# Split f32r operands in ten first products of an attention and feed-forward kernel, with low parts added by DMA

## The chip, the core and the metric

The kernel runs on one core of a Trainium2 chip. The metric is the device time of one launch in microseconds, the median of several runs. The engines are TensorE (PE, matmuls; PEld its weight loads), VectorE (DVE), ScalarE (ACT), GpSimd (POOL) and SyncE (SP), which only issues DMAs here. Each engine works through its own instructions in order and waits on semaphores for the others.

## What is computed

The reference runs three stages on 1536 tokens (two batches of 768) of width 512:

```python
scores = scale * np.matmul(q, k.transpose(0, 1, 3, 2)) + bias     # 8 heads, local window of 96 and 8 global keys
attn = softmax(where(keep, scores, -1e9)) @ v
x = attn as (1536, 512)
h = x @ w_in                                                      # 512 -> 2048
g = h * np.tanh(np.log1p(np.exp(h)))                              # above 20: log1p(exp(h)) = h
x = g @ w_out                                                     # 2048 -> 512
for e in range(4):                                                # experts, p normalised over e
    out += p[:, e:e + 1] * (np.maximum(x @ w1[e], 0.0) @ w2[e])
```

The first feed-forward weights `w_in` and `w_out` arrive as 64-bit numbers.

## The kernel before

The tokens are worked on in three blocks of 512. Block 0 passes attention, the first feed-forward layer (FFN) and most of the experts; blocks 1 and 2 do their attention in between and follow. The change lies in block 0's FFN.

That FFN has 16 steps of 128 hidden channels. Step `s` needs its weights: SP loads 1 MB of 64-bit words into one of four buffers (`fetch`; `big0`, `big1`, and `raw0`, `raw1`, which hold attention inputs at other times), ACT takes the absolute value of the upper words, scaled (L603), and three DVE instructions put a 32-bit number together (L606, L608, L610). The result is a tile `w` of 128x1024: columns 0 to 511 for the first product, 512 to 1023 for the second. SP also stores it to `wfirst` in HBM for later blocks. The first product `hidden_first` (L771) multiplies f32 operands: four blocks of 128 rows, x in the tile `x0`, into a PSUM bank `h`; in the trace an f32 matmul appears as two, so one product is 8 rows. The gate follows: exponent on ACT (L660), cap on DVE (L664), square, logarithm and exponential on ACT (L668, L673, L674), and three DVE instructions (L679, L683, L687) that leave the gated values in `gl` or `gh`. The second product `project_first` (L784) adds them through `w` into the banks `acc0` to `acc3`; the last two steps share one such projection. All this is f32. Later FFN blocks and the experts split operands into a high part rounded to f32r and a low part, and take three f32r products: high by high, high by low, low by high (L644, `hidden`).

The order of all this is a string of letters, `PLAN`, written out by hand. One letter is one instruction or a few, and each engine carries out its own in the order of the string. `t` is one of the three DVE instructions of a conversion (48 letters), `a` ACT's first instruction of one, `H` a first product, `e c n l u v g` the parts of a gate, `P` a projection and `Q` the last one, of steps 14 and 15. `i` loads four attention inputs of block 1, `j` splits queries and keys, `1` to `6` are the pieces of the attention of block 1 for one pair of heads (2 scores, 3 softmax, 4 scaling and splitting of later inputs, 5 transpose, 6 product with the values), and `w` is a third of the splitting of expert weights (a high part on ACT, two low parts). `TURN` names the buffer of each step's load. A load is issued as soon as the step that used its buffer before has been converted, and takes its place in SP's queue.

After `Q`, the results go into y0 and step 16, the first expert, begins.

Of the kernel before, what the change touches and what calls it, by code (L numbers as in the profile page):

```python
# [9 lines left out]
F32 = mybir.dt.float32  # L10
F32R = mybir.dt.float32r
I32 = mybir.dt.int32
I64 = mybir.dt.int64
AF = mybir.ActivationFunctionType
ALU = mybir.AluOpType

P = 128
B, H, S, D = 2, 8, 768, 64
# [4 lines left out]
TB = 512  # L23
NB = NTOK // TB
KC = DM // P
NF1 = 16
# [15 lines left out]

PLAN = (
    "SSYXXESYSEXSEDXNXESNTDCTXSENAZNEXATTSCZEDAXANSFSNEXTTDCNEZAXANTETSCZaADXNAtSFNTEXSCTXEAZSEDAVSVaXTTX"
    "CSEZAEADVVFTXTCEZAAaDVVTtTCaAZtAFtHttttHetctntlHtauevgHcattnltPeuvagcetPntltauHvgctntlPteauvgHctntlt"
    "aPuevgctnPtltauvHgttatPectntltHauvgtPetctnltHtauvgaHtectntlHteauvgPcetntltHwuvgctnPtltieuvHgcwnwlPeu"
    "vgcnljHwjuvgwP12ecnlwHuvg34612Pecnl3uvg5Hw4w6w12Pecnl3uvg54P6Q"
)

AFTER = {  # L50
# [2 lines left out]
}  # L53


TURN = [0, 1, 2, 3] * (NF1 // 4)
FREE = {2: 4, 3: 8}
EXTRA = 15,

# [99 lines left out]
class Pair:  # L159
# [17 lines left out]
    def split(self):  # L177
        pass
# [361 lines left out]
class Body:  # L540
# [35 lines left out]
    def fetch(self, s):  # L576

        kind, t, n = self.steps[s]
        if kind == "ffn" and self.wide and t == 0:
            self.w64[s] = (self.big + self.twice)[TURN[n]].bitcast(I64)  # L580
            if n > 0 or not self.loaded:
# [185 lines left out]

    def hidden_first(self, s):
        self.h[s] = ps = self.bank(f"h{s}")
        for kc in range(KC):  # L770
            self.nc.tensor.matmul(ps, self.w32[s][:, kc * P:(kc + 1) * P], self.x0[:, kc, :], start=kc == 0, stop=kc == KC - 1)  # L771

    def gate_first(self, s):
        self.g[s] = self.temp("gl" if s % 2 else "gh", s, bufs=3)
# [254 lines left out]
    def first_block(self, ready, now):  # L1029


        nc = self.nc
        pairs = [FirstPair(self, k) for k in range(TB // P * NP)]
        then = Attention(self, self.pair, 1, NB - 1)
        n = dict.fromkeys("SXEDNTCAFHecnluvgPatw", 0)
        narrowing = [self.narrow(c) for c in range(NF1)]
        parts = [self.part(c) for c in range(NF1, NF1 + 3)]
        self.x0 = self.xy.tile([P, KC, TB], F32, tag="xyh", name="x0")

        for pair in pairs:  # L1040
            pair.load()
# [3 lines left out]
        def ahead():  # L1045
            while ready["fetch"] < NF1:
                c = ready["fetch"]
                before = [m for m in range(c) if TURN[m] == TURN[c]][-1:]
                if n["S"] < FREE.get(TURN[c], 0) or any(n["t"] < 3 * m + 3 for m in before):
                    break  # L1050
                now("fetch", c + 1)
# [24 lines left out]
            return run  # L1076

        def hidden(s):
            if s == 10:
                for c in range(NF1, NF1 + 3):  # L1080
                    self.fetch(c)
            assert n["F"] == 4 and n["t"] >= 3 * s + 3
            self.accumulating = True
            self.hidden_first(s)
            ahead()
            self.nc.sync.dma_start(self.wfirst[s], self.w32[s])
# [4 lines left out]
        def last(k):  # L1091
            assert n["P"] == NF1 - 2 and n["g"] == NF1
            self.project_first(NF1 - 2, NF1 - 1)

        def begin(c):
            assert (c < 2 or n["A"] >= min(2 * c - 2, len(pairs))) and (c < 10 or n["P"] > c - 10)
            next(narrowing[c])
# [7 lines left out]
        def part(k):  # L1105
            c, third = divmod(k, 3)
            assert ready["fetch"] >= NF1 and n["S"] == len(pairs) and n["P"] >= 8 + 2 * c
            if third == 0:
                ready["fetch"] = NF1 + 3
                next(parts[c])  # L1110
            try:
                parts[c].send("vector" if third else None)
            except StopIteration:
                pass

        def begin_next(k):
            assert n["t"] == 3 * NF1
            then.load(4)

        pair = lambda stage, *args: lambda k: getattr(pairs[k], stage)(*args)  # L1120
# [1 line left out]
            "S": scores, "X": pair("biased"), "E": pair("exps"), "D": inverse, "N": scale(nc.gpsimd), "V": scale(nc.vector), "T": pair("trans"),  # L1122
            "C": pair("copy", nc.scalar.copy), "Z": pair("copy", nc.vector.tensor_copy), "A": pair("av"),
            "F": take(nc.scalar.copy), "G": take(nc.vector.tensor_copy), "a": begin, "t": convert, "w": part,
            "Y": warm, "H": hidden, "e": self.mish_exp, "c": self.mish_cap, "n": self.mish_n, "l": self.mish_r,
            "u": self.mish_u, "v": self.mish_v, "g": self.gate_first, "P": project, "Q": last,
            "i": begin_next, "j": lambda k: then.split(k + 1),
            "1": lambda k: then.ahead(), "2": lambda k: then.scores(), "3": lambda k: then.softmax(),
            "4": lambda k: (then.norm(), then.parts()), "5": lambda k: then.trans(), "6": lambda k: then.av(),
        }  # L1130
# [199 lines left out]
```

## Time and profile before

| | |
|---|---|
| median of 3 runs | 883.1 us (882.48 to 883.12) |
| profiled execution | 882.74 us, span 880.9 us |
| PE busy | 869.7 us of the span (99%) |
| DVE, ACT, POOL busy | 569.9, 482.3, 388.6 us |
| first product of step 0 to end of `Q` | 37.5 to 150.4 us |
| chain of work that ended last | PE 94% of the span |

Shares of the whole span are means over unlike stages: DVE is at 65% overall and at 98% in the stretch of the changed steps. The granted clock of PE is 1.00 (of 2.4 GHz) in every window read here.

### The profile page before, as it was taken

The page shows a single profiled execution, that of the slowest core. Times are in us where ns is not written, and L with a number is a line of the kernel's source. Part 1 is how long each engine was busy: PE and PEld are TensorE (multiplying, and loading weights), DVE is VectorE, ACT ScalarE, POOL GpSimd, SP SyncE. Part 2 cuts the span into 40 slices and gives each one's busy share as a digit, 9 for nine tenths or more (in the row PEclk, how much of TensorE's full clock was granted, in tenths as well). Part 3 has the DMA queues.
Part 4 walks back from the last instruction along what each step waited for, and adds up shares of the span by engine and source line. Part 5 has one row for each costly group of instructions (what it writes and reads, how often), then busy time and mean ns, then how long its engine had stood idle before and what let it go on. Part 6 is the DMA issues. An engine that isn't in the chain of part 4 may idle for free.

```text
span 880.9 us, 11248 instructions
## 1 busy us (share of the span) xinstructions
PE 869.7 (99%) x3848; PEld 669.2 (76%) x3848; DVE 569.9 (65%) x1112; ACT 482.3 (55%) x943; POOL 388.6 (44%) x416
## 2 busy tenths in 40 slices
PE   9899999999999999999999999999999999999997
PEld 5544445888888888888888888788888888888886
DVE  6999977866678674566656667645455555555555
ACT  6665665878777775577675567533333333333330
POOL 4000020777777776555310225554445555544420
PEclk9999999999999999999999999999999999999999
DMA  9488834444435432887555640611111112111002
GB/s 323 168 330 257 320 127 148 143 147 169 164 126 183 148 143 73 308 291 288 221 197 195 244 168 0 185 56 49 48 48 48 48 54 65 50 48 48 1 1 99
DMA packets 39858, 126.15 MB, mean 143 GB/s; under 512 B 4080, under 2 KB 6896, under 8 KB 37744
## 3 DMA queue, kind: packets, MB, share of 16 engines
q1 hardware_dynamic: 39648, 125.32, 40.6%
q8 instruction: 32, 0.52, 0.2%
q14 instruction: 34, 0.28, 0.1%
q10 hardware_dynamic: 144, 0.02, 0.0%
HBM read 97.02 MB, written 28.31 MB: 142 GB/s over the span
## 4 chain that ended last, share of the span: by engine, by line
PE 94%; DVE 2%; DMA 1%; ACT 0%; POOL 0%; issue 0%; ACTq 0%; POOLq 0%; DVEq 0%
PE acc_l L944 20%; PE h L644 20%; PE acc L732 20%; PE ha L893 9%; PE hx L893 7%; PE h L771 6%; PE acc L784 6%; PE pt L201 2%; PE o L308 2%; PE s L262 1%; PE s L261 1%; DMA qk<-in_qk 1%; PE s L365 0%; PE o L403 0%; DVE raw L843 0%; DVE t3l L822 0%
## 5 line engine op out<-in xcount | busy, mean ns | idle before, releaser
L629 POOL TENSOR_TENSOR wl<-w,wh 128x512 fp32r<-128x512 f32 x90 | 118.7, 1339 | 59.9 <-ACT wh L626 57.4
L797 DVE SCALAR_TENSOR_TENSOR big<-acc_l,prob,big 128x512 f32<-128x512 f32 x120 | 88.8, 746 | 79.0 <-PE acc_l L944 78.8
L876 POOL TENSOR_TENSOR zl<-wout,zh 128x512 fp32r<-128x512 f32 x32 | 40.8, 1297 | 85.1 <-ACT zh L874 85.1
L876 POOL TENSOR_TENSOR sumsl<-bias,sumsh 128x512 fp32r<-128x512 f32 x32 | 42.9, 1364 | 69.2 <-ACT sumsh L874 69.2
L679 DVE SCALAR_TENSOR_TENSOR nr<-e,n 128x512 f32<-128x512 f32 x48 | 33.1, 690 | 48.3 <-ACT n L674 48.3
L906 ACT COPY raw<-ha 128x512 f32<-128x512 f32 x33 | 19.4, 587 | 79.6 <-PE ha L893 79.6
L660 ACT ACTIVATE e<-h 128x512 f32<-128x512 f32 x48 | 28.1, 586 | 61.1 <-PE h L644 25.5
L196 POOL TENSOR_SCALAR p<-p,st 128x256 f32<-128x256 f32 (+1 forms) x58 | 42.0, 735 | 39.9 <-ACT v L250 35.0
L771 PE MATMUL h<-x,w 128*128 128x512 f32 x128 | 56.8, 593 | 0.7 <-ACT x L408 0.7
L732 PE MATMUL acc<-wh,gh 128*128 128x512 f32 x128 | 52.5, 410 | 0.0
L286 ACT ACTIVATE p<-t,st 128x256 f32<-128x256 f32 (+1 forms) x96 | 46.3, 484 | 8.1 <-DVE st L275 8.0
L944 PE MATMUL acc_l<-zh,gh 128*128 128x512 f32 x128 | 50.7, 396 | 0.0
L626 ACT CAST wh<-w 128x1024 fp32r<-128x1024 f32 x48 | 50.2, 1046 | 0.7
L644 PE MATMUL h<-y0h,wh 128*128 128x512 f32 x128 | 50.6, 395 | 0.0
L944 PE MATMUL acc_l<-zh,gl 128*128 128x512 f32 x128 | 50.5, 394 | 0.0
L944 PE MATMUL acc_l<-zl,gh 128*128 128x512 f32 x128 | 50.4, 394 | 0.0
L644 PE MATMUL h<-y0l,wh 128*128 128x512 f32 x128 | 50.3, 393 | 0.0
L732 PE MATMUL acc<-wh,gl 128*128 128x512 f32 x128 | 50.2, 392 | 0.0
L644 PE MATMUL h<-y0h,wl 128*128 128x512 f32 x128 | 50.2, 392 | 0.0
L944 PE MATMUL acc_l<-zh,gl_late 128*128 128x512 f32 (+1 forms) x128 | 50.0, 391 | 0.0
L275 DVE CUSTOM_DVE_ANT_0 t<-s,bias 128x256 f32<-128x256 f32 (+1 forms) x96 | 34.5, 399 | 24.0 <-PE s L262 20.8
L944 PE MATMUL acc_l<-zh,gh_late 128*128 128x512 f32 (+1 forms) x128 | 50.0, 391 | 0.0
(232 smaller groups left out, 2489.7 us busy)
## 6 DMA issues: line engine op xcount, KB each, us to landing
w<-in_wts SPq DMA_DIRECT2D x32, 512.0 KB, 4.6
raw<-in_qkv SPq DMA_DIRECT2D x32, 512.0 KB, 3.6
big<-in_wff SPq DMA_DIRECT2D x8, 1024.0 KB, 6.8
raw<-in_wff SPq DMA_DIRECT2D x8, 1024.0 KB, 8.2
wfirst<-w SPq DMA_DIRECT2D x16, 512.0 KB, 8.1
w<-wfirst SPq DMA_DIRECT2D x16, 512.0 KB, 4.5
wkeep<-wh SPq DMA_DIRECT2D x16, 512.0 KB, 3.6
wkeep<-wl SPq DMA_DIRECT2D x16, 512.0 KB, 2.9
```

What stands on the lines that cost most here:

```text
L196: engine.tensor_scalar(self.p[:, j, 0:self.nk * P], self.p[:, j, 0:self.nk * P], st[:, 2 + j:3 + j], 0.0, ALU.mult, ALU.add)
L286: nc.scalar.activation(p[:, j, 0:n], t[:, j, 0:n], AF.Exp, bias=self.least[:, j:j + 1], scale=-1.0, accum_out=self.sum[:, j:j + 1])
L626: (nc.vector.tensor_copy if copy == "vector" else nc.scalar.copy)(hi, w)
L629: getattr(nc, engine or "gpsimd").tensor_tensor(lo[:, c], w[:, c], hi.bitcast(F32)[:, c], ALU.subtract)
L644: nc.tensor.matmul(ps, a[:, c], r[:, kc, :], start=m == 0, stop=m == 3 * KC - 1)
L732: nc.tensor.matmul(acc[:, h], a, r, start=opens and k == 0 and m == 0, stop=closes and k == len(chunks) - 1 and m == 2)
L771: self.nc.tensor.matmul(ps, self.w32[s][:, kc * P:(kc + 1) * P], self.x0[:, kc, :], start=kc == 0, stop=kc == KC - 1)
L784: self.nc.tensor.matmul(acc, w[k][:, 512 + d * P:512 + (d + 1) * P], g[k], start=s == 0, stop=s == NF1 - 1)
L797: nc.vector.scalar_tensor_tensor(o, acc, p, o, ALU.mult, ALU.add)
L876: nc.gpsimd.tensor_tensor(lo[:, c], w[:, c], hi.bitcast(F32)[:, c], ALU.subtract)
L893: nc.tensor.matmul(ps, a[:, c], r[:, kc, :], start=opens and n == 0, stop=n == 5, skip_group_check=True)
L944: nc.tensor.matmul(o, a[:, c], r[:, w], start=n == 0, stop=n == 5)
```

## The change

From step `WHOLE` = 6 on, the first product takes split operands. x is split once: for each of its four blocks ACT copies the high part (`x0h`) and DVE subtracts it from x (`x0l`); letters `b`, eight. For each of steps 6 to 15 the first half of `w` is split by letter `s`: ACT writes minus w, rounded to f32r, into a tile half `halfl`; a DMA issued from POOL adds w itself to that tile in place, which leaves the low part; ACT writes the rounded w into `halfh`. There are four such slots, so step `s` takes the one of step `s` - 4. The product is then 12 f32r matmuls in place of four f32 ones, with the low part of the weights in the last four.

```diff
-TURN = [0, 1, 2, 3] * (NF1 // 4)
+TURN = [0, 1, 2, 3] * 3 + [0, 1] * 2
+WHOLE = 6
...
     def hidden_first(self, s):
         self.h[s] = ps = self.bank(f"h{s}")
-        for kc in range(KC):
-            self.nc.tensor.matmul(ps, self.w32[s][:, kc * P:(kc + 1) * P], self.x0[:, kc, :], start=kc == 0, stop=kc == KC - 1)
+        w = self.w32[s]
+        if s < WHOLE:
+            for kc in range(KC):
+                self.nc.tensor.matmul(ps, w[:, kc * P:(kc + 1) * P], self.x0[:, kc, :], start=kc == 0, stop=kc == KC - 1)
+            return
+        (wh, wl), (xh, xl), m = self.halves[s % KC], self.x[0], 0
+        for a, r in ((wh, xh), (wh, xl), (wl, xh)):
+            for kc in range(KC):
+                self.nc.tensor.matmul(ps, a[:, kc * P:(kc + 1) * P], r[:, kc, :], start=m == 0, stop=m == 3 * KC - 1)
+                m += 1
+
+    def split_first(self, s):
+
+        nc, w, (wh, wl) = self.nc, self.w32[s][:, 0:512], self.halves[s % KC]
+        nc.scalar.activation(wl, w, AF.Copy, scale=-1.0)
+        nc.gpsimd.dma_start(wl.bitcast(F32), w, accum_op=ALU.add)
+        nc.scalar.copy(wh, w)
...
+        self.x[0] = self.block("x0")
+        halves = [self.xy.tile([P, KC, TB], F32R, tag="xyl", name=f"half{p}") for p in "hl"]
+        self.halves = [[half[:, k, :] for half in halves] for k in range(KC)]
...
-            if s == 10:
+            if s == 9:
                 for c in range(NF1, NF1 + 3):
                     self.fetch(c)
...
+        def x_part(k):
+            assert n["F"] == 4
+            (xh, xl), at = [x[:, k // 2, :] for x in self.x[0]], self.x0[:, k // 2, :]
+            if k % 2:
+                nc.vector.tensor_tensor(xl, at, xh.bitcast(F32), ALU.subtract)
+            else:
+                nc.scalar.copy(xh, at)
...
-                parts[c].send("vector" if third else None)
+                parts[c].send("vector" if third and c < 1 else None)
...
-            assert n["t"] == 3 * NF1
+            assert n["t"] >= 36
             then.load(4)
...
+            "b": x_part, "s": split,
```

`PLAN` is written anew as well. Four of the six low parts of letter `w` go from DVE to POOL. Steps 12 to 15 load into `big0` and `big1` in turn, so that `raw0` and `raw1` are free for block 1's attention inputs after step 11. Three places show what the new order moves.

DVE, around the gate of step 4 (`gh` in L687 before, L688 now). The conversion that stands there (`w_696` before, `w_701` now) is that of step 7; `x0l` is the low part of x. Before:

```order
L664 TENSOR_SCALAR n_722<-e_721 128x512
L606 TENSOR_SCALAR w_696<-w_696 128x1024
L608 SCALAR_TENSOR_TENSOR w_696<-raw_123,w_696 128x1024
L610 SCALAR_TENSOR_TENSOR w_696<-raw_123,w_696 128x1024
L679 SCALAR_TENSOR_TENSOR nr_751<-e_721,n_722 128x512
L683 SCALAR_TENSOR_TENSOR nr_751<-nr_751,n_722 128x512
L687 SCALAR_TENSOR_TENSOR gh_757<-nr_751,h_700 128x512
```

Now:

```order
L1118 TENSOR_TENSOR x0l<-x_173,x0h 128x512
L665 TENSOR_SCALAR n_727<-e_726 128x512
L1118 TENSOR_TENSOR x0l<-x_173,x0h 128x512
L607 TENSOR_SCALAR w_701<-w_701 128x1024
L680 SCALAR_TENSOR_TENSOR nr_755<-e_726,n_727 128x512
L684 SCALAR_TENSOR_TENSOR nr_755<-nr_755,n_727 128x512
L1118 TENSOR_TENSOR x0l<-x_173,x0h 128x512 x2
L688 SCALAR_TENSOR_TENSOR gh_770<-nr_755,h_705 128x512
L609 SCALAR_TENSOR_TENSOR w_701<-raw_123,w_701 128x1024
L611 SCALAR_TENSOR_TENSOR w_701<-raw_123,w_701 128x1024
```

Four subtractions of x stand among these, and two of the conversion's instructions have moved behind the gate.

ACT, at the gates of steps 14 and 15 (`e_1057` and `e_1119` before, `e_1165` and `e_1196` now), with the attention of block 1 around them: `p` is an exponential, `pt` the copy of a transpose, `qs`, `kh` and `v` casts of later inputs, `wh` an expert weight. Before:

```order
L660 ACTIVATE e_1057<-h_1015 128x512
L668 ACTIVATE e_1057<-n_1058 128x512
L673 ACTIVATE n_1058<-e_1057 128x512
L674 ACTIVATE n_1058<-n_1058 128x512
L286 ACTIVATE p_1_1064,st_1_1066<-t_1_1065,st_1_1066 128x256 x2
L298 CAST pt_0_1081<-pt_0_1076 128x4x128
L626 CAST wh_1090<-w_871 128x1024
L235 CAST qs_3_1097<-raw_123 128x256
L237 CAST kh_3_1099<-raw_123 128x512
L250 CAST v_1_1104<-raw_122 128x2x2x64
L660 ACTIVATE e_1119<-h_1084 128x512
```

Now:

```order
L661 ACTIVATE e_1165<-h_1127 128x512
L669 ACTIVATE e_1165<-n_1166 128x512
L674 ACTIVATE n_1166<-e_1165 128x512
L675 ACTIVATE n_1166<-n_1166 128x512
L236 CAST qs_2_1176<-raw_123 128x256
L238 CAST kh_2_1178<-raw_123 128x512
L251 CAST v_0_1183<-raw_122 128x2x2x64
L661 ACTIVATE e_1196<-h_1151 128x512
L669 ACTIVATE e_1196<-n_1197 128x512
L674 ACTIVATE n_1197<-e_1196 128x512
L675 ACTIVATE n_1197<-n_1197 128x512
L287 ACTIVATE p_1_1208,st_1_1210<-t_1_1209,st_1_1210 128x256 x2
```

Before, the exponentials of pair 1 and the copy of pair 0's transpose stood between the two gates; now those exponentials stand behind both. On PE the order from there on is first product 14, first product 15, a score, projection 12, transpose of pair 0, projection 13, a score, transpose of pair 1, the product with the values, `Q`. Before, first products 14 and 15 had a score, projection 11 and a transpose between them.

SP, from the load of step 13 on (`big` and `raw` from `in_wff` are the loads of steps, `w` from `in_wts` those of experts, `raw` from `in_qkv` attention inputs). Before, `raw_122` and `raw_123` from `in_wff` are steps 14 and 15:

```order
L582 DMA big_125<-in_wff 128x1024
L582 DMA raw_122<-in_wff 128x1024
L1086 DMA wfirst<-w_696 128x1024
L582 DMA raw_123<-in_wff 128x1024
L1086 DMA wfirst<-w_724 128x1024
L1086 DMA wfirst<-w_745 128x1024
L587 DMA w_867<-in_wts 128x1024
L587 DMA w_869<-in_wts 128x1024
L587 DMA w_871<-in_wts 128x1024
```

Now, the last `big_124` and `big_125` are steps 14 and 15:

```order
L583 DMA big_125<-in_wff 128x1024
L1105 DMA wfirst<-w_701 128x1024
L1105 DMA wfirst<-w_729 128x1024
L588 DMA w_893<-in_wts 128x1024
L588 DMA w_895<-in_wts 128x1024
L588 DMA w_897<-in_wts 128x1024
L1105 DMA wfirst<-w_757 128x1024
L230 DMA raw_122<-in_qkv 128x1024 x2
L230 DMA raw_123<-in_qkv 128x1024 x2
L583 DMA big_124<-in_wff 128x1024
L1105 DMA wfirst<-w_773 128x1024
L583 DMA big_125<-in_wff 128x1024
```

The loads of the last two steps have gone behind the expert weights and the attention inputs. On POOL eight of the ten adding DMAs stand ahead of everything else of this stretch, and the last two (steps 14 and 15) behind the splitting of two queries and keys.

## Rows read from the trace of the kernel before

**Rows 1.** The page, busy us and share of the span by engine.
```profile
PE 869.7 (99%) x3848; PEld 669.2 (76%) x3848; DVE 569.9 (65%) x1112; ACT 482.3 (55%) x943; POOL 388.6 (44%) x416
```
**Rows 2.** Windows: PE, PEld, DVE, ACT, POOL busy us; clock, DMA share, GB/s.
```profile
75.00:100.00 25.00, 25.00 (x60) 11.12 (x59) 24.45 (x32) 14.18 (x19) 0.00 (x0) 1.00 0.90 295
100.00:125.00 25.00, 25.00 (x62) 11.31 (x62) 21.09 (x29) 14.73 (x25) 4.92 (x4) 1.00 0.59 212
```
**Rows 3.** Timeline of PE: start, duration, instruction, count; first f32, then f32r.
```profile
75.36 3.60 PE L771 MATMUL h<-x,w 128*128 128x512 f32 x8
78.79 3.60 PE L784 MATMUL acc<-gl,w 128*128 128x512 f32 x8
...
168.41 0.39 PE L644 MATMUL h<-y0h,wh 128*128 128x512 f32 x1
...
171.17 0.28 PE L261 MATMUL s<-kh,qs 128*128 128x256 f32 x1
```
**Rows 4.** Timeline of DVE: gate of step 4, cap, conversion, gate of step 5.
```profile
68.88 0.69 DVE L679 SCALAR_TENSOR_TENSOR nr<-e,n 128x512 f32<-128x512 f32 x1
...
70.93 0.42 DVE L664 TENSOR_SCALAR n<-e 128x512 f32<-128x512 f32 x1
71.26 0.69 DVE L606 TENSOR_SCALAR w<-w 128x1024 int32<-128x1024 int32 x1
...
74.39 0.68 DVE L679 SCALAR_TENSOR_TENSOR nr<-e,n 128x512 f32<-128x512 f32 x1
...
75.83 0.69 DVE L687 SCALAR_TENSOR_TENSOR gl<-nr,h 128x512 f32<-128x512 f32 x1
```
**Rows 5.** Groups by shape, 0 to 265 us: count, busy us, mean ns, idle before.
```profile
L626 ACT CAST wh<-w 128x1024 fp32r<-128x1024 f32 x19 | 20.0, 1050 | 0.4
L242 DVE TENSOR_TENSOR kl<-raw,kh 128x512 fp32r<-128x512 f32 x20 | 16.6, 831 | 0.6
L237 ACT CAST kh<-raw 128x512 fp32r<-128x512 f32 x22 | 13.6, 620 | 0.0
L299 DVE TENSOR_TENSOR pt<-pt,pt 128x512 fp32r<-128x512 f32 x16 | 11.1, 691 | 11.6 <-ACT pt L298 11.6
L668 ACT ACTIVATE e<-n 128x512 f32<-128x512 f32 x16 | 10.1, 630 | 24.1 <-DVE n L664 24.1
L660 ACT ACTIVATE e<-h 128x512 f32<-128x512 f32 x16 | 9.5, 591 | 11.4 <-PE h L771 11.1 <-DVE nr L679 0.3
...
L196 DVE TENSOR_SCALAR p<-p,st 128x256 f32<-128x256 f32 x6 | 1.9, 351 | 0.1
```
**Rows 6.** Timeline of DVE: cap and last gate instruction of step 15.
```profile
138.51 0.42 DVE L664 TENSOR_SCALAR n<-e 128x512 f32<-128x512 f32 x1
...
142.41 0.69 DVE L687 SCALAR_TENSOR_TENSOR gl<-nr,h 128x512 f32<-128x512 f32 x1
```
**Rows 7.** Timeline of PE: product 15, projection 12, a transpose, the last projection.
```profile
131.67 3.60 PE L771 MATMUL h<-x,w 128*128 128x512 f32 x8
...
135.58 3.60 PE L784 MATMUL acc<-gh,w 128*128 128x512 f32 x8
139.01 0.60 PE L201 MATMUL pt<-ident,p 128*128 128x128 f32 x4
...
143.35 1.02 PE L784 MATMUL acc<-gh,w 128*128 128x512 f32 x2
```
**Rows 8.** DMA issues at 68.5, 92 and 102 us: KB each, median us to landing.
```profile
raw<-in_wff SPq DMA_DIRECT2D x1, 1024.0 KB, 7.3
...
wfirst<-w SPq DMA_DIRECT2D x2, 512.0 KB, 12.3
...
raw<-in_qkv SPq DMA_DIRECT2D x4, 512.0 KB, 4.8
```
**Rows 9.** Timelines of POOL and DVE where both work; idle before in brackets.
```profile
117.42 0.89 POOL L240 TENSOR_TENSOR qs<-raw,qs 64x256 fp32r<-64x256 f32 x1 [93.66 <-DMA wfirst<-w]
...
117.75 1.11 DVE L683 SCALAR_TENSOR_TENSOR nr<-nr,n 128x512 f32<-128x512 f32 x1
```

More of the change, by code (lines that the diff above doesn't have):

```diff
@@ L44 @@
     "SSYXXESYSEXSEDXNXESNTDCTXSENAZNEXATTSCZEDAXANSFSNEXTTDCNEZAXANTETSCZaADXNAtSFNTEXSCTXEAZSEDAVSVaXTTX"
-    "CSEZAEADVVFTXTCEZAAaDVVTtTCaAZtAFtHttttHetctntlHtauevgHcattnltPeuvagcetPntltauHvgctntlPteauvgHctntlt"
-    "aPuevgctnPtltauvHgttatPectntltHauvgtPetctnltHtauvgaHtectntlHteauvgPcetntltHwuvgctnPtltieuvHgcwnwlPeu"
-    "vgcnljHwjuvgwP12ecnlwHuvg34612Pecnl3uvg5Hw4w6w12Pecnl3uvg54P6Q"
+    "CSEZAEADVVFTXTCEZAAaDVVTtTCaAZtAFtHtbtttHetctntlHtauevgHecattnltPuvagectnPtltauHvgctntlPteausvgbHcbn"
+    "bltbuaPvbbebgtaPtcsttnHltusvegcPtntltauHsvgtPteactnltHtsuvaHgtecstPtnltieusHvgctntlPteusvHgcnlwHauve"
+    "jgPcetntltajHusvgctP12ntlteusPvgwwcnl3HwwwuvgHecnl4612Peuvgcnl3uvgwww546P123546Q"
 )
@@ L1034, in first_block @@
         then = Attention(self, self.pair, 1, NB - 1)
-        n = dict.fromkeys("SXEDNTCAFHecnluvgPatw", 0)
+        n = dict.fromkeys("SXEDNTCAFHecnluvgPatwbs", 0)
         narrowing = [self.narrow(c) for c in range(NF1)]
@@ L1078, in hidden @@
         def hidden(s):
-            if s == 10:
+            if s == 9:
                 for c in range(NF1, NF1 + 3):
                     self.fetch(c)
-            assert n["F"] == 4 and n["t"] >= 3 * s + 3
+            assert n["F"] == 4 and n["t"] >= 3 * s + 3 and (s < WHOLE or n["b"] == 2 * KC and n["s"] > s - WHOLE)
             self.accumulating = True
@@ L1093, in last, with split @@
             self.project_first(NF1 - 2, NF1 - 1)
+        def x_part(k):
[5 more added lines that the diff above has]
+                nc.scalar.copy(xh, at)
+        def split(k):
+            s = WHOLE + k
+            assert n["t"] >= 3 * s + 3 and (k < KC or n["H"] > s - KC)
+            self.split_first(s)
         def begin(c):
```

## The prediction

> **What bounds the kernel now.** I read the page first, then the windows of 25 us, then the timelines of TensorE (PE), VectorE (DVE) and ScalarE (ACT) between 37 and 150 us, then the DMA landings. On the page PE is busy for 869.7 of 880.9 us [rows 1]. The changed steps lie between 37 and 150 us. There the windows show PE at 25.00 of 25, but DVE at 24.45 of 25 until 100 us and 21.09 in the next window, with the DMA engines at 0.90 and 0.59 [rows 2]. So PE sets the time here, with DVE a hair behind it: DVE has 0.6 us to spare in one window and 3.9 in the next. A microsecond off PE is worth a microsecond only if DVE, ACT and the loads come along. Behind this block PE is full again, so what the block gains or loses arrives at the end.
>
> In the trace a first product of 8 f32 matmuls lasts from 75.36 to 78.79, 3.43 us. A product of 12 f32r matmuls of the same size lasts from 168.41 to 171.17, 2.76 us [rows 3].
>
> **The change, part by part.**
>
> *PE.* Ten steps (6 to 15) go from 3.43 to 2.76 us: 10 x 0.67 = **6.7 us less**. This is the whole offer, 0.76% of the time.
>
> *Splitting x.* Four copies on ACT and four subtractions on DVE are new. One such subtraction, 128x512, took 0.69 us (L299 [rows 5]). All four stand on DVE ahead of the gate of step 5, as the order shows. Before, that gate starts at 75.83 and takes 0.69, so it ends at 76.52, and PE wants it at 78.79 [rows 3, 4]: 2.3 us to spare. Now the gate ends 4 x 0.69 = 2.8 us later, less an estimated 0.3 because records of neighbours overlap a little (three of 0.69 take 2.05 from 68.88 to 70.93 [rows 4]), and up to 0.7 more, since an ACT copy (0.59 for 128x512, L660 [rows 5]) stands ahead of step 4's chain, for which DVE waits: 76.52 + 2.5 + 0.7 = 79.7. PE, with its first short product, arrives at 75.36 + 2.76 = 78.1. It waits **1.6 us** (1.0 to 1.9). Afterwards DVE needs 5.5 us per step (from 68.88 to 74.39 [rows 4]: 2.05 for the gate's three instructions, 0.33 for the cap, 3.13 for the conversion) against 3.43 + 2.76 = 6.2 on PE, so it gains on PE again and the ACT copies of the split, 2 x 0.59 per step, fit beside them.
>
> *The last steps.* Steps 14 and 15 now stand back to back on PE. Both gate chains, and the attention pieces between them, must pass before the transpose of attention pair 1, which PE meets ahead of the last projection. PE from the end of first product 14 to that transpose: product 15 (2.76), score (0.48), projection 12 (3.43), transpose (0.43), projection 13 (3.43), score (0.48) = 11.0 us. The 0.48 is 135.58 - 131.67 - 3.43, and 143.35 - 139.01 holds 3.43 + 0.43 + 0.48 [rows 7]. The other chain: exponent of step 14 (0.59); from its cap to the end of its gate 4.6, as from 138.51 to 142.41 + 0.69 [rows 6], and inside it now two casts on ACT (0.62 or less each, together about 1.0) and the low part of a key on DVE (0.83), 1.85 together; the same 4.6 for step 15; then ACT's weight cast (1.05) and copy of a transpose, of which about 0.5 show; the subtraction on DVE (0.69); the scaling of the pair (2 x 0.35 and some 0.36 for two short instructions) [rows 5]. Sum 0.6 + 6.45 + 4.6 + 0.5 + 0.7 + 1.05 = 13.9, less 0.4 of seams: 13.5. PE waits **2.5 us** (1.5 to 3.5). Before, the two products had a projection and more between them, and the last gate ended at 142.41 + 0.69 = 143.10 for a projection at 143.35 [rows 6, 7]: just in time.
>
> *Low parts on POOL.* Four subtractions of a weight's low part leave DVE for POOL. Where POOL worked beside DVE (from 117.42) a DVE instruction that else takes 0.69 took 1.11 [rows 9]. One or two such meetings lie on the chain above: **+0.4 us** (0 to 0.8).
>
> *The adding DMAs.* Ten, of 256 KB each; no row shows one. In the rows a 1 MB load that had the queue to itself landed after 7.3 us, 512 KB of attention inputs after 4.8, and stores at the end of a long queue after 12.3 [rows 8]. POOL's queue is empty from 24 to 117 us (its next instruction had been idle 93.66 us [rows 9]), so nothing stands ahead of the first eight. The room: PE reads the low weights only in the last third of a product. For step 7: from the end of its conversion DVE does a cap, a conversion and a gate (0.33 + 3.13 + 2.05), then PE a projection and two thirds of a product (3.43 + 1.84), 10.8, less 0.6 for the negating copy: some 10.2 us. For step 14 the DMA stands on POOL behind two key splits, and its room is about 8.5, an estimate from the same durations. I take the lone loads as nearest, 4.8 to 7.3 us, since a DMA from POOL stands in a queue of its own: cost **0**. At 12.3 it would be 3.8 at step 14 and about 2 each at steps 7 and 10, nearly 8 us.
>
> One price stands only on a page: the Trainium skill, "DMA: Bandwidth & Descriptors", section "Anatomy of one DMA — SWDGE (gpsimd) path", gives 2.0 us plus the bytes over 436 GB/s for a DMA that POOL issues; that would be an estimated 2.6 us here, no run shows it, and by it the sum keeps its 0.
>
> *Loads.* Steps 14 and 15 now reuse the buffers of 12 and 13. Their loads are issued only when those are converted, and on SP behind three weight loads, a store and four attention loads; before, they stood ahead of all these. From the end of conversion 12 to ACT's first use of load 14 lie on DVE two gates, two caps and a conversion (4.1 + 0.7 + 3.1) and on ACT three of 0.63 and a cast of 1.05 [rows 4, 5]: 10.8 us of room. Landings range from 7.3 alone to 12.3 at the end of a queue [rows 8], and five adding DMAs share those engines. ACT works in order, so a late load moves the chain of the last steps one for one. Cost 0 to 5; I take **0.7**, near the low end, since DMA has free time before the queue forms (0.90 busy, 295 GB/s, in 75 to 100 us [rows 2]).
>
> *Sum:* -6.7 + 1.6 + 2.5 + 0.4 + 0 + 0.7 = **-1.5 us**. The profiled execution took 882.74 us (span 880.9), which gives 881.2. The median of the runs is 883.1, 0.36 above it, which gives **881.6 us**.
>
> **The rivals.**
>
> *A, the forecast:* three of the four parts of the gain go into waits on DVE and ACT; 880 to 883.
>
> *B, all of it arrives:* DVE and ACT have no chain as long as I count and PE never waits: 883.1 - 6.7 = 876.4, up to 880 with one of the two waits left. For it: PE waits nowhere in this block before. Against it: DVE's 0.6 us to spare, against 2.8 of new subtractions.
>
> *C, the adding DMAs land late (slower):* DMA engines 0.90 busy, and the added values are read as well as written. It decides at about 10 us from the negating copy to landing, where step 14's wait of 10 - 8.5 eats the 1.5; above 10.2 each microsecond costs 3 (steps 7, 10 and 14). At 10.5 us: 2.0 + 2 x 0.3 = 2.6, time 884.2; at 12.3, 7.8 and 889.
>
> *D, POOL can't issue while DVE runs:* POOL and DVE did slow each other, 0.69 to 1.11 [rows 9], and DVE leaves 0.6 us free in 25 [rows 2]. If POOL had to wait for one to three DVE instructions per DMA, at 0.69 to 1.25 each, up to 3.5 us would be added to 7.3: 10.8, which costs about 3.5, so 885. The page of the Trainium skill "SBUF — State Buffer", section "SBUF: two separate sides", says so: a DMA from POOL stalls because descriptors can't be written while DVE holds the shared port. The collision in [rows 9] agrees with a lock between compute instructions; no run here shows it for a DMA.
>
> *E, loads 14 and 15 late:* landing 3 to 5 us beyond their room, moved one for one: 883.1 - 2.2 + 3 to 5 = 884 to 886. For it: the queue ahead of them holds 4 MB, and 12.3 us was seen at such a queue.
>
> **How the numbers follow.** Chances: A 0.45, B 0.10, C 0.19, D 0.08, E 0.18. About what a measurement can tell here is 0.2%, 1.8 us: faster is below 881.3, slower above 884.9. A lies half on either side of 881.3 (0.22 faster, 0.23 same). B is faster. C and D are slower for 0.20 and same for 0.07. E is slower for 0.11, same for 0.05, faster for 0.02. Sums: faster 0.34, same 0.35, slower 0.31. The range goes from 878.5 (a third of B) to 887.5 (most of C, D and E) and leaves out about 0.15. A's own range is 880 to 883.
>
> **What would show it.** First products at 2.76 us from step 6 show the offer. A's mark is PE idle of 1 to 2 us ahead of projection 5, put to DVE, and of 2 to 3 ahead of the second attention transpose of the block, with none between. C and D: PE idle ahead of the last four matmuls of a product, put to a DMA of POOL's queue, with landings above 9 us; D alone if POOL issues late. E: ACT idle ahead of the load's first read for steps 14 or 15. Wrong would be the whole working if PE waits in neither place, or if the f32r products take as long as the f32 ones beside f32 projections.

## The result, and the profile of the changed kernel

The changed kernel takes 889.68 us (889.2 to 891.02) against 882.98 (882.48 to 883.12) for the kernel before on the same chip: ratio 1.0079, interval 1.0062 to 1.0097, so **6.7 us slower** where 1.5 us faster was forecast, and above the top of the forecast's range (887.5). The profiled execution has a span of 887.4 us (880.9 before).

On the page PE has fewer busy microseconds than in [rows 1], and the chain that ended last is no longer nearly all PE (94% before):

```profile
PE 866.6 (98%) x3888; PEld 677.1 (76%) x3888; DVE 572.9 (65%) x1112; ACT 494.3 (56%) x967; POOL 402.8 (45%) x430
...
PE 83%; DVE 10%; ACT 3%; issue 2%; DMA 2%; POOL 0%; DVEq 0%; ACTq 0%
```

The windows, with columns as in [rows 2], say where. Up to 125 us PE loses little, but from 125 to 150 it is busy for 16.89 of 25 us; and in the four shorter windows the granted clock falls to 0.50, the lower of its two levels (1.2 of 2.4 GHz), after a window in which PE did almost nothing:

```profile
75.00:100.00 25.00, 23.56 (x81) 14.82 (x80) 24.38 (x32) 18.99 (x32) 5.18 (x6) 1.00 0.99 330
100.00:125.00 25.00, 25.00 (x86) 15.41 (x85) 19.29 (x23) 17.30 (x29) 7.63 (x6) 1.00 0.88 303
125.00:150.00 25.00, 16.89 (x58) 10.08 (x57) 19.82 (x41) 14.88 (x34) 7.70 (x7) 0.87 0.24 71
...
136.00:140.00 4.00, 3.77 (x12) 1.67 (x10) 3.90 (x8) 1.11 (x3) 0.94 (x1) 1.00 0.40 127
140.00:144.00 4.00, 0.17 (x2) 0.00 (x0) 2.41 (x5) 3.94 (x10) 0.36 (x1) 0.93 0.01 4
144.00:148.00 4.00, 1.40 (x6) 1.11 (x7) 3.79 (x7) 1.17 (x4) 2.87 (x3) 0.50 0.09 10
148.00:152.00 4.00, 4.00 (x10) 2.05 (x10) 2.65 (x10) 3.36 (x11) 0.66 (x1) 0.71 0.34 121
```

PE's timeline names the waits. The number in brackets is the idle time ahead of an instruction and what ended it:

```profile
80.10 3.70 PE L800 MATMUL acc<-gl,w 128*128 128x512 f32 x8 [1.44 <-DVE gl L688]
...
95.28 3.59 PE L800 MATMUL acc<-gl,w 128*128 128x512 f32 x8
...
101.45 2.73 PE L800 MATMUL acc<-gh,w 128*128 128x512 f32 x6
...
134.99 0.81 PE L202 MATMUL pt<-ident,p 128*128 128x128 f32 x4 [1.45 <-DVE p L197]
...
139.46 0.36 PE L262 MATMUL s<-kh,qs 128*128 128x256 f32 x1 [0.23 <-DVE gh L688]
...
146.33 0.47 PE L202 MATMUL pt<-ident,p 128*128 128x128 f32 x1 [6.16 <-DVE p L197]
147.08 0.90 PE L202 MATMUL pt<-ident,p 128*128 128x128 f32 x3 [0.27 <-DVE p L197]
...
148.63 1.85 PE L800 MATMUL acc<-gh,w 128*128 128x512 f32 x2
150.32 1.02 PE L800 MATMUL acc<-gl,w 128*128 128x512 f32 x2
...
155.93 0.80 PE L645 MATMUL h<-y0h,wh 128*128 128x512 f32 x1
```

The products are as short as offered: from one projection to the next 101.45 - 95.28 = 6.17 us, 3.43 + 2.74. Of the forecast's two waits, the one before projection 5 is there at 1.44 us, but the last steps hold 1.45 + 0.23 + 6.16 + 0.27 = 8.1 us in place of 2.5. The last projection starts at 148.63, against 143.35 in [rows 7], with two matmuls in 1.69 us (148.63 to 150.32) that took 0.86 before.

ACT met both late loads, and the chain of waits runs from the first of them to that transpose without touching PE (start, duration, engine and what):

```profile
111.11 1.14 ACT L604 ACTIVATE w<-big 128x1024 f32<-128x1024 f32 x1 [2.81 <-DMA big<-in_wff]
...
116.61 1.18 ACT L604 ACTIVATE w<-big 128x1024 f32<-128x1024 f32 x1 [0.71 <-DMA big<-in_wff]
```

```profile
97.53 13.55 DMA big<-in_wff
...
113.83 1.66 DVE w L609
115.51 2.21 DVE w L611
...
131.56 0.50 ACT e L661
132.08 1.13 DVE n L665
...
146.20 0.83 DVE p L197
147.08 0.90 PE pt L202 x3
```

Two parts of this chain are longer than usual, each beside an instruction of POOL. The conversion's instructions at 113.83 and 115.51 took 1.66 and 2.21 us, where those of the next conversion took 1.23 each, while POOL split a key. The scaling of pair 1 (two instructions, 0.62 us together for pair 0) took 1.85 while POOL formed low parts:

```profile
114.47 2.17 POOL L243 TENSOR_TENSOR kl<-raw,kh 128x512 fp32r<-128x512 f32 x1
...
143.64 2.49 POOL L630 TENSOR_TENSOR wl<-w,wh 128x512 fp32r<-128x512 f32 x2 [6.32 <-ACT wh L627]
```

```profile
145.17 1.85 DVE L197 TENSOR_SCALAR p<-p,st 128x256 f32<-128x256 f32 x2
```

### The profile page after: what moved, and what is told of

It reads as the page before. It is cut to its first block, busy times and chain, and to the rows that moved or that the text cites. A ratio compares the mean times of both kernels' runs of the same rounds, so it can differ in the third digit from the quotient of the medians.

```text
span 887.4 us, 11396 instructions
## 1 busy us (share of the span) xinstructions
PE 866.6 (98%) x3888; PEld 677.1 (76%) x3888; DVE 572.9 (65%) x1112; ACT 494.3 (56%) x967; POOL 402.8 (45%) x430
## 4 chain that ended last, share of the span: by engine, by line
PE 83%; DVE 10%; ACT 3%; issue 2%; DMA 2%; POOL 0%; DVEq 0%; ACTq 0%
PE acc_l L960 20%; PE h L645 20%; PE acc L733 19%; PE ha L909 9%; PE hx L909 7%; DVE w L609 2%; PE pt L202 2%; PE o L309 2%; DVE w L611 2%; DMA big<-in_wff 2%; ACT p L287 1%; PE acc L800 1%; DVE w L607 1%; DVE nr L684 1%; DVE nr L680 1%
## 5 line engine op out<-in xcount | busy, mean ns | idle before, releaser
L630 POOL TENSOR_TENSOR wl<-w,wh 128x512 fp32r<-128x512 f32 x94 | 123.7, 1336 | 73.1 <-ACT wh L627 70.6
L733 PE MATMUL acc<-wl,gh 128*128 128x512 f32 x128 | 50.0, 390 | 0.0
```

The source lines that it names most:

```text
L630: getattr(nc, engine or "gpsimd").tensor_tensor(lo[:, c], w[:, c], hi.bitcast(F32)[:, c], ALU.subtract)
L733: nc.tensor.matmul(acc[:, h], a, r, start=opens and k == 0 and m == 0, stop=closes and k == len(chunks) - 1 and m == 2)
```

## The experiments

Three theories for the lost time: **L**, the loads of steps 14 and 15 come late, and ACT, working in order, carries that to the end; **P**, POOL's new low parts slow DVE's chain; **O**, the order of the last steps alone. Later a fourth came up: the fall of the granted clock.

### Loads first, low parts back on DVE, no adding DMAs, products alone

The expert weights are fetched at step 12, so that loads 14 and 15 stand ahead of them on SP (the first high copy of `w` moves with them):

```diff
-            if s == 9:
+            if s == 12:
                 for c in range(NF1, NF1 + 3):
```

> The changed kernel, except that SP issues the three expert weight loads behind the loads of steps 14 and 15 and not ahead of them, and the first split of an expert weight on ACT stands later. Theory L (the loads of steps 14 and 15 land late, and ACT, which works in order, carries that into the last gates): the two loads land 4 us or more earlier than 13.6 and 13.5 us after issue, ACT's waits of 2.81 and 0.71 us for them go, PE's wait ahead of the transpose of pair 1 falls from 6.2 us to about 3, its clock stays up: 884 to 886.5 us. Theory P (POOL beside DVE lengthens DVE's chain of the last steps): the waits on ACT go, but DVE still ends the chain late: 888 to 889.5. Theory O (the order of the last steps alone): no change, 889.7.

Measured: 886.12 us (885.75 to 887.25; ratio 1.0037, interval 1.0023 to 1.0051), 3.6 below the changed kernel. The loads land 8.7 us after issue, where they took 13.5, and ACT doesn't wait for them. L is borne out for 3.6 us. But PE still waits 5.8 us at the transpose, where about 3 was expected, and the clock still falls (0.50 from 140 to 148 us):

```profile
143.31 0.47 PE L202 MATMUL pt<-ident,p 128*128 128x128 f32 x1 [5.77 <-DVE p L197]
```

All low parts of expert weights back on DVE:

```diff
-                parts[c].send("vector" if third and c < 1 else None)
+                parts[c].send("vector" if third else None)
```

> The changed kernel with the four low parts of expert weights on DVE again, as before the change, and not on POOL. Theory P: the DVE instructions of 1.23, 1.23 and 1.85 us that ran beside POOL at 133, 137 and 145 us take 0.17, 0.69 and 0.62 again; that gives back 3 us and costs 2.6 us for the four subtractions, two of which stand behind the last gate: 887.5 to 890, with these rows short again. Theory L or O: the subtractions are only added to the chain: 891 to 892.5.

Measured: 892.64 us (892.07 to 894.15; ratio 1.0114, interval 1.0097 to 1.0131), 3.0 above the changed kernel. As the net cause P falls: in this order moving them to POOL helps.

The adding DMAs left out, so that the low parts stay minus the weights:

```diff
-        nc.gpsimd.dma_start(wl.bitcast(F32), w, accum_op=ALU.add)
```

> The changed kernel without the ten adding DMAs, so the low parts of the weights are left as minus the weights. Theory L with the adding DMAs as its cause: the loads of steps 14 and 15 land some 3 us sooner, ACT's waits of 2.81 and 0.71 us go, 885 to 887 us. Theory L with the order of the loads alone as its cause: they land 13 us after issue as before, 889 to 890.

Measured: 886.53 us (886.2 to 887.0; ratio 1.0044, interval 1.0027 to 1.0061), 3.2 below the changed kernel. The loads of steps 14 and 15, in their late place, now land after 7.8 us. DMA issues at 95 to 106 us, the changed kernel and then this one (columns as in [rows 8]):

```profile
big<-in_wff SPq DMA_DIRECT2D x2, 1024.0 KB, 13.5
...
halfl<-w POOLq DMA_DIRECT2D x3, 256.0 KB, 8.3
```

```profile
big<-in_wff SPq DMA_DIRECT2D x2, 1024.0 KB, 7.8
```

No PE wait of the changed kernel is put to an adding DMA. Their price is paid by other transfers. It is the same 3 us as with the loads moved ahead: late place and adding DMAs cost only together, since with either one gone ACT no longer waits for a load.

The products on constant operands in the order of the kernel before, with no split at all; four writes of the constants on POOL stand ahead of step 0.

```diff
         def hidden(s):
+            if s == 0:
+                for tile_ in list(self.x[0]) + halves:
+                    self.nc.gpsimd.memset(tile_.bitcast(F32), 0.01)
```

> The kernel before, in its own order, with f32r products from step 6 on whose split operands are constants set once on POOL: nothing is split, no DMA is added. If PE alone set the time of this block, 6.7 us go: 876.3. If the chains of DVE and ACT bind as soon as PE is faster, PE waits ahead of projection 6 (some 1 us), ahead of the first scores (1 us) and of a later score (2 to 3 us), and only 1 to 3 us arrive: 880 to 882.

Measured: 888.92 us (887.38 to 890.76; ratio 1.0077, interval 1.0057 to 1.0096), a miss of the experiment: the block began at 43.42 us in place of 37.49. Only the stretch from the first product to step 16 can be read: 111.3 us (43.42 to 154.73) against 112.3 (37.49 to 149.82). Of the 6.7 us 1.0 arrives, with waits of 0.8, 0.8, 0.6 and 2.0 us, three of them put to DVE.

### The order by itself, and the clock

The changed kernel's order with f32 products and no splits (the letters `b` and `s` are gone from `PLAN`):

```diff
-WHOLE = 6
+WHOLE = 16
```

> The changed kernel's order with all sixteen first products left in f32: the letters for the splits of x and of the weights are taken out, and with them the four subtractions on DVE, the copies on ACT and the adding DMAs. The place of the loads, the order of the last steps and the low parts of expert weights on POOL stay as in the changed kernel. It gives the price of the new order by itself. If the order alone carries the loss, it stands about 3 to 6 us above the kernel before (886 to 889) and PE still waits several us before the transpose of pair 1. If the loss needs the splits and their DMAs (late loads through busy DMA engines), the loads of steps 14 and 15 land after about 8 us as without the adding DMAs, ACT doesn't wait for them, and PE, 6.7 us later than with the short products, waits little: 883 to 885.

Measured: 888.7 us (888.46 to 888.92; ratio 1.0066, interval 1.0049 to 1.0082). With none of the new products and splits the order costs 5.7 us. PE's waits, 3.37 and 0.41 us at the transpose of pair 1, then a clock of 0.78:

```profile
145.99 0.33 PE L202 MATMUL pt<-ident,p 128*128 128x128 f32 x1 [3.37 <-DVE p L197]
146.73 0.90 PE L202 MATMUL pt<-ident,p 128*128 128x128 f32 x3 [0.41 <-DVE p L197]
```

The transpose comes at 145.99 with slow products and at 146.33 with fast ones, but that they are so close is chance. Here no load is late, and ACT takes the exponent of step 14 when the slow product allows it:

```profile
130.99 0.60 ACT L661 ACTIVATE e<-h 128x512 f32<-128x512 f32 x1 [0.98 <-PE h L774]
```

In the changed kernel the product ends at 126.58, and the late loads hold the exponent back to 131.46. From the exponent to the transpose it is 15.0 us here and 14.9 there.

The kernel before, f32 and its own loads, with only the last steps in the new order (products 14 and 15 back to back, the exponentials of pair 1 behind gate 15):

```diff
-    "vgcnljHwjuvgwP12ecnlwHuvg34612Pecnl3uvg5Hw4w6w12Pecnl3uvg54P6Q"
+    "vgcnljHwjuvgwP12Pecnl3HwuvgHecnl4612Peuvgcnl3uvgwww546P123546Q"
```

> The kernel before, f32 products, its loads and its low parts on DVE; only the last steps, from the gate of step 13 on, stand in the order of the changed kernel: products 14 and 15 back to back and the exponentials of attention pair 1 behind the gate of step 15. No split, no adding DMA, no late load. If this order of the last steps is what costs (the f32 kernel with the whole new order stood 5.7 us above the kernel before), PE waits 3 to 4 us before the transpose of pair 1, put to DVE, and the time is 886 to 889. If it was the rest of the new order (low parts on POOL, the loads, the earlier letters), PE waits less than 1 us there and the time is 882.5 to 884.

Measured: 887.6 us (886.12 to 888.4; ratio 1.0052, interval 1.0034 to 1.007): 4.9 us from the order of the last steps alone, with low parts on DVE. PE waits once:

```profile
145.55 1.16 PE L201 MATMUL pt<-ident,p 128*128 128x128 f32 x4 [2.85 <-DVE p L196]
```

ACT takes the exponent of step 14 at 131.05, as soon as its product allows; 14.5 us pass from there to the transpose. The wait is 2.85 of the 4.9 us. Behind it the granted clock falls here too:

```profile
144.00:148.00 4.00, 2.45 (x9) 2.03 (x10) 3.48 (x11) 0.77 (x4) 0.72 (x1) 0.71 0.40 131
```

```profile
147.36 1.90 PE L784 MATMUL acc<-gh,w 128*128 128x512 f32 x2
...
154.71 0.80 PE L644 MATMUL h<-y0h,wh 128*128 128x512 f32 x1
```

The last projection lasts 7.35 us (147.36 to 154.71) where it took 6.47 in the kernel before (143.35 to 149.82), and from the transpose to it 1.81 us pass, against 1.12 with the clock at 1.00 (the kernel with the gates first, below). That is 1.6 us more. O is shown, for f32 products.

The fall of the clock: seven f32 matmuls on a zero operand in the changed kernel's idle time, ahead of that transpose:

```diff
+            "z": lambda k: nc.tensor.matmul(self.acc[0][1], self.zero, self.g[14], start=False, stop=False),
```

> The changed kernel with seven f32 matmuls of 128x512 on a zero operand (0.86 us each, 6 us together; they add zero to the results) ahead of the transpose of pair 1, where PE stood idle for 6.2 us. They do no work that counts. If PE's idle only shows as waiting, the time stays at 889.7, or rises by what the filling lasts beyond the wait (0 to 0.5). If the fall of the granted clock to 0.50 after that idle costs time of its own, the clock stays at 1.00 from 140 to 152 us, the last projection takes 6.5 us in place of 7.3, and the time falls by 1.5 to 2 us, to 887.7 to 888.2.

Measured: 887.82 us (887.41 to 888.55; ratio 1.0053, interval 1.0036 to 1.007), 1.9 below the changed kernel, though PE does 6 us more. The chain still ends at 147 to 148 us, but the clock stays at 1.00 and the last projection takes 6.5 us again:

```profile
140.86 6.17 PE L1163 MATMUL acc<-gh,zero 128*128 128x512 f32 x14
147.20 0.33 PE L202 MATMUL pt<-ident,p 128*128 128x128 f32 x1 [0.17 <-DVE p L197]
147.93 0.55 PE L202 MATMUL pt<-ident,p 128*128 128x128 f32 x3 [0.41 <-DVE p L197]
...
148.79 1.02 PE L800 MATMUL acc<-gh,w 128*128 128x512 f32 x2
149.65 1.02 PE L800 MATMUL acc<-gl,w 128*128 128x512 f32 x2
...
155.25 0.80 PE L645 MATMUL h<-y0h,wh 128*128 128x512 f32 x1
```

So the fall of the clock costs 1.9 us by itself, by the medians (no run of this kernel is as slow as any of the changed one). In the two profiled executions the stretch from the second part of that transpose to step 16 shows 1.5: 7.32 us (147.93 to 155.25) against 8.85 (147.08 to 155.93).

### Can the 6.7 us be collected?

On top of the kernel with the loads first, the last steps in the order of the kernel before:

```diff
-    "gPcetntltajHusvgctP12ntlteusPvgwwwcnl3HwwwuvgHecnl4612Peuvgcnl3uvgwww546P123546Q"
+    "gPcetntltajHusvgctP12ntlteusvgwcnlwwHuvg34612Pecnl3uvg5Hw4w6w12Pecnlwww3uvg54P6Q"
```

> The kernel with the two loads first (886.1), and from the gate of step 12 on the order of the kernel before: first products 14 and 15 apart, with a score, projection 11 and a transpose between them, each pair's exponentials ahead of the next gate. If the order of the last steps is what leaves 5.8 us of waiting there, the wait before the transpose of pair 1 falls below 2 us, the granted clock stays at 1.00 through 150 us, and the time falls by 3 to 6 us, to 880 to 883. If the chain of DVE and ACT is as long in either order, the wait only moves (to projections 12 and 13 or the product with the values), and the time stays at 885 to 887.

Measured: 886.02 us (885.0 to 886.71; ratio 1.0034, interval 1.002 to 1.0048), no change, against the expectation of O. The wait moved to three places, the largest now before the last projection:

```profile
145.57 1.80 PE L800 MATMUL acc<-gl,w 128*128 128x512 f32 x2 [2.85 <-DVE gl L688]
```

DVE's timeline shows why the gate is late: beside POOL's low parts (137.95 to 141.07) the subtraction for a key took 1.64 us (0.69 in the changed kernel, at 136.03) and the cap of step 15 took 1.49 (0.42 in [rows 6]):

```profile
138.30 1.64 DVE L243 TENSOR_TENSOR kl<-raw,kh 128x512 fp32r<-128x512 f32 x1
139.87 1.49 DVE L665 TENSOR_SCALAR n<-e 128x512 f32<-128x512 f32 x1
```

Part of this wait is thus POOL's. But two kernels with all low parts on DVE wait at the same place in this order of the last steps, 2.03 us (products alone) and 2.04 (the next one): it has room for products of 3.43 us, not for shorter ones.

The order and loads of the kernel before throughout, the splits set into it, and x's low part formed by four adding DMAs as well:

```diff
-TURN = [0, 1, 2, 3] * 3 + [0, 1] * 2
+TURN = [0, 1, 2, 3] * (NF1 // 4)
...
             if k % 2:
-                nc.vector.tensor_tensor(xl, at, xh.bitcast(F32), ALU.subtract)
+                nc.scalar.activation(xl, at, AF.Copy, scale=-1.0)
+                nc.gpsimd.dma_start(xl.bitcast(F32), at, accum_op=ALU.add)
```

> The order and the loads of the kernel before throughout, with the splits set into it; the low part of x is formed as that of the weights is (ACT writes minus x, a DMA adds x), so that DVE has nothing new at all, and the low parts of expert weights stay on DVE. PE is offered 6.7 us. If nothing but the new order and DVE's four subtractions cost time, all of it comes: 876 to 878. If DVE's and ACT's gate chains bind as soon as PE is faster, most of it goes into waits of PE at gates, put to DVE, and 880 to 883 is left. If the fourteen adding DMAs make the loads late, ACT waits for loads of steps 9 to 13 and it is 884 or more.

Measured: 898.84 us (897.24 to 900.0; ratio 1.0181, interval 1.0164 to 1.0198). It is slower, but not through late loads (ACT waits 1.1 us for one): PE waits 13.2 us for the adding DMAs themselves, six of which are issued between 65 and 81 us:

```profile
92.69 0.80 PE L779 MATMUL h<-x0l,halfh 128*128 128x512 f32 x1 [6.80 <-DMA x0l<-x]
```

They landed 9.1 to 11.9 us after issue, as in rival C. They were also issued late: the third of x only at 75.91, though its input was ready at 72.2:

```profile
75.91 0.88 POOL L1119 DMA_DIRECT2D x0l<-x  x1 [5.80 <-ACT e L669]
```

DVE wasn't what held this one up, as D would have it: DVE itself stood idle from 72.31 to 73.77. From the fourth of these DMAs on, each was issued 0.2 to 0.3 us after the one three places ahead of it had landed, so that never more than three were under way. What sets this, no run shows.

Loads first, the gates of 14 and 15 ahead of attention's pieces, all low parts on DVE, those of the second and third expert weight behind the last gate:

```diff
-    "gPcetntltajHusvgctP12ntlteusPvgwwwcnl3HwwwuvgHecnl4612Peuvgcnl3uvgwww546P123546Q"
+    "gPcetntltaHusvgctP12ntlteusvgwcnlHeuvgwwjcnlP3Huvgec46nl12P3uvg5P4612www35w46wwQ"
```

> The split products with the two loads first, and the last steps ordered so that the gates of 14 and 15 go ahead of the attention pieces: exponent 14 right behind product 14, the scaling of pairs, the expert weights' splits and the pair's exponentials behind the gates, the key split behind the split of step 15; all low parts of expert weights on DVE, behind the last gate. DVE still subtracts for x, so 1.4 us of waiting before projection 5 stay. If the chain of gates in the last steps is what sets the end, PE waits less than 2 us in the last steps, the clock stays at 1.00, and the first expert product starts 2 to 4 us earlier than in the kernel before (149.8): 879 to 881. If the chain is as long in any order, it stays at 885 to 887.

Measured: 883.53 us (883.21 to 883.89; ratio 1.001, interval 1.0 to 1.002), 2.6 below the kernel with the loads first, but short of the 879 to 881 expected. The last projection starts at 141.85 with the clock at 1.00, but PE waits 0.66 and 1.22 us at the two transposes ahead of it, and step 16 then waits 1.13 us for y0.

The same, with x's low parts by adding DMAs as in the run above, but spread over 38 to 57 us (the letters `b` go behind `H` and `P` of the first steps):

> As the kernel with the gates first, and the low parts of x formed by ACT and four adding DMAs issued between 38 and 52 us, spread out and long before step 6, so that DVE has no subtraction for x. If those 2.8 us of DVE cost PE the 1.4 us before projection 5, they come back: no wait there, and 1 to 1.5 us less than the kernel with the gates first (878 to 880). If DVE, at 98% busy, binds a few steps later all the same, or ACT's four more copies delay gates, the time doesn't change by more than 0.5 us. If the adding DMAs slow the loads of steps 4 to 8, ACT waits for loads and it is slower.

Measured: 882.25 us (881.96 to 882.51; ratio 0.9994, interval 0.9984 to 1.0003), 1.3 less; the wait before projection 5 is gone. So x's subtractions on DVE cost about what PE waited there, 1.4.

The last projection ahead of the transpose of pair 1, the third expert weight split behind y0:

```diff
-    "gPcetntltaHusvgctP12ntlteusvgwcnlHeuvgwwjcnlP3Huvgec46nl12P3uvg5P4612www35w46wwQ"
+    "gPcetntltaHusvgctP12ntlteusvgwcnlHeuvgwwjcnlP3Huvgec46nl12P3uvgP54612www3Q546www"
```

> As the kernel with x by DMA (882.25), with the last projection ahead of the transpose of pair 1 and the product with the values, the transpose of pair 0 behind projection 13, and the third expert weight split only behind the copies to y0. There PE waited 0.86 and 1.22 us for the scaling of pairs and 1.14 us for y0, whose copies stood behind expert weights on ACT and DVE. If the order of the last steps still holds back part of the offer, those three waits go and the time falls by 1.5 to 3 us, to 879 to 881, below the kernel before. If the gate of step 15 is next in line, PE waits for it ahead of the last projection and the time stays at 882 to 883.

Measured: 883.13 us (882.29 to 884.34; ratio 1.0005, interval 0.9996 to 1.0014), a miss. Step 16 starts at 145.47, 4.35 us earlier than in the kernel before, and then PE waits behind DVE's queue:

```profile
152.73 1.19 PE L309 MATMUL o<-pt,v 128*128 128x256 f32 x4 [3.09 <-DVE of L329]
```

That split put into a gap of DVE ahead of y0:

```diff
-    "gPcetntltaHusvgctP12ntlteusvgwcnlHeuvgwwjcnlP3Huvgec46nl12P3uvgP54612www3Q546www"
+    "gPcetntltaHusvgctP12ntlteusvgwcnlHeuvgwwjcnlP3Huvgec46nl12P3uvgP54612wwww3wwQ546"
```

> As the kernel with the last projection first (883.13), with the third expert weight split in the gap that DVE had ahead of the copies to y0 (1.28 us), in place of behind them. There PE stood 3.09 us before the product with the values of pair 1, behind DVE's queue, with the granted clock at 0.50 after it. If DVE's queue past the last projection is what now holds the offer back, that wait shrinks by about 1.3 us, the fall of the clock with it, and the time goes to 880.5 to 881.8, below the kernel before. If DVE is simply full, the wait turns up elsewhere and the time stays at 882.5 to 883.5.

Measured: 881.8 us (880.76 to 882.29; ratio 0.9986, interval 0.9977 to 0.9995). That wait is 1.88 us, the clock stays at 1.00. This version is 7.9 us below the changed kernel and 1.1 below the kernel before (882.42 to 883.36 on that chip, so the two ranges don't meet).

The same order with f32 products and no splits:

> The order of the kernel with the third expert weight split in the gap, with all first products left in f32 and without any split of x or of the weights' first halves and without adding DMAs: what that order gives without the change's products. If the split products still earn something once the order lets them, this stands 2 us or more above the kernel with the splits (883 to 885). If the gain is the order's own, both stand within 1 us of each other.

Measured: 886.73 us (885.12 to 887.34; ratio 1.0039, interval 1.0025 to 1.0053), above the 883 to 885 expected. In an order made for them the split products earn 4.9 of their 6.7 us; but that order costs f32 products 3.8, so only 1.1 is left against the kernel before.

## Why the prediction was wrong

**PE's offer: right.** 6.17 us from projection to projection against 6.86 before; the f32r products take 2.74 us beside f32 projections.

**Splitting x: right.** 1.6 forecast, 1.44 measured at the place named, 1.3 to be had back.

**The last steps: the step that failed.** The forecast set two chains side by side from the end of product 14: PE 11.0 us, gates and attention 13.5 (13.9 with its 0.4 for POOL), difference 2.5. The mechanism is the right one: with f32 products and nothing else changed it gives 2.85 us (last steps alone), and PE's side took 11.1 with the loads first. Two things were mis-sized. The chain is 14.9 us from the exponent of step 14, not 13.9. And the exponent doesn't start when the product ends. With the loads first the product ends at 126.42, where product 15 starts, and ACT comes to the exponent at 128.43, since it has gate 13, a pair's exponentials and a weight cast ahead of it: 2.0 us.

```profile
126.42 1.07 PE L779 MATMUL h<-x0h,halfh 128*128 128x512 f32 x4
```

```profile
128.43 0.58 ACT L661 ACTIVATE e<-h 128x512 f32<-128x512 f32 x1
```

With the forecast's 2.5 and 0.4, and 1.0 for the length, this gives 5.9, and 5.77 was measured. In the changed kernel the exponent comes at 131.46, 4.9 us after the product.

**Loads: rival E, mis-sized.** 0.7 us was taken from a range of 0 to 5; two runs put it at 3.2 to 3.6, one for one with the 3.5 us that ACT waited, as E said. The room was right (10.8 forecast, 13.55 - 2.81 = 10.7 measured). The landing was not: 13.5 us, outside the 7.3 to 12.3 of [rows 8]. The forecast had seen the adding DMAs share the engines, but costed them at nothing. Without them the load lands in 7.8 us.

**Adding DMAs: right on their own waits, wrong on those of others.** The room of 10.2 us held (the first eight landed after 7.4 to 10.0), so C didn't happen in the changed kernel; in five of the later kernels PE waited 0.6 to 0.9 us in all for adding DMAs. D didn't either: with DVE busy for 4.90 of 5 us POOL issued a DMA in about 1 us, and the two at 120.6 and 125.1 landed after 3.4:

```profile
120.00:125.00 5.00, 5.00 (x19) 2.87 (x18) 4.90 (x7) 3.29 (x6) 1.66 (x2) 1.00 0.34 68
```

```profile
halfl<-w POOLq DMA_DIRECT2D x2, 256.0 KB, 3.4
```

The Trainium skill, "SBUF — State Buffer", section "SBUF: two separate sides", describes a stall of a DMA from POOL while DVE runs an instruction in a two-port mode. No such stall shows here; whether DVE's instructions there are of that kind, no run shows. The estimate of 2.6 us from the Trainium skill, "DMA: Bandwidth & Descriptors", section "Anatomy of one DMA — SWDGE (gpsimd) path", compares with 3.4 at a DMA share of 0.34 and with 7.4 to 10.0 for the first eight (share 0.99 from 75 to 100 us).

**Low parts on POOL: mis-sized, but small in the net.** The forecast's 0.4 was for one or two meetings of 0.4 us. On the chain there were two, of 0.7 and 1.2: the cap of step 14 took 1.13 us in place of 0.42, the scaling of pair 1 took 1.85 in place of 0.62. Without these 1.9 us the chain would be 13.0, below the forecast's 13.5. On DVE the low parts cost 3.0 us more still (low parts back on DVE).

**The clock: missing.** 1.9 us. No row of the kernel before showed it, as PE waits nowhere in this block there.

From start to start of PE's instructions the account closes. The block began 0.3 us later (37.81) and took 118.1 us up to step 16 in place of 112.3: 5.8 longer. Counted in this way, the wait before projection 5 cost 1.8 us, the one for pair 0's transpose 1.8, the one at a score 0.5, those for the two parts of pair 1's transpose 6.3 and 0.6, and the clock 1.5. These are 12.5 us, of which the offer (10 x 0.69 = 6.9, from projection to projection) takes back all but 5.6, nearly the whole 5.8. They are more than the idle times because a product that is followed by a wait shows its whole length (75.34 to 78.66 before projection 5, 3.3 us in place of 2.74).

## What to carry to other kernels

Before counting a faster step as a gain, follow the chain of the other engines to its end with its true starting point, which is when the engine in order gets to the first instruction, not when its input is ready. An order written out by hand is made for the durations it had: test a new order with the old operation alone, since that shows at once that the order has a price (5.7 us here); what else holds the new operation up, such as late loads, it doesn't show. And a DMA that nobody waits for is not free if a load that somebody waits for shares its engines.

## What the runs showed of the hardware that was not expected

- After PE had stood idle for 6.16 us its granted clock was 0.50 in the window from 144 to 148 us, and 0.71 in the next; filling that idle time with work on zeros gave 1.9 us back.
- An adding DMA of 256 KB landed after 3.4 us at a DMA share of 0.34 and after 7.4 to 10.0 in the busy stretch (share 0.99 from 75 to 100 us). With the ten of them the 1 MB loads of steps 14 and 15 landed after 13.5 us, without them after 7.8.
- POOL's DMAs in close order came late: of six issued within 16 us no more than three were under way at a time, they landed after 9.1 to 11.9 us, and PE waited 13.2 us for them. For the four of x spread over 18 us, long before their use, it didn't wait.
- Beside a POOL instruction a short DVE instruction can take several times as long: the cap of 0.42 us took 1.49 beside the low parts of a weight.
